# Converting stored fp64 weights with fewer steps, with their range checked in later blocks and one set of operands made later

## The chip, the cores and the metric

The kernel runs on one core of a Trainium2 chip. The metric is the time of one execution in microseconds (us) of the device. The core has TensorE (PE, matmuls; PEld is its weight load), VectorE (DVE), ScalarE (ACT), GpSimd (POOL) and SyncE (SP), whose queue issues every DMA of this kernel. Each engine works through its own instructions in the order in which they stand.

## The reference

A linear attention with a decaying state feeds an MLP with squared ReLU, and that feeds a mixture of eight experts which are all computed and weighted by a Sinkhorn-normalised gate:

```python
for t in range(S):                                   # 4 batches x 8 heads, S=768, D=48
    state = f[:, :, t, :, None] * state + np.einsum('bhd,bhe->bhde', k[:, :, t], v[:, :, t])
    y[:, :, t] = np.einsum('bhd,bhde->bhe', q[:, :, t], state)
...
h = x @ w_in                                         # 3072 tokens, 384 -> 2048
r = np.maximum(h, 0.0)
return (r * r) @ w_out                               # 2048 -> 384
...
P = np.exp(logits - logits.max())                    # logits = x @ w_gate, 8 columns
for _ in range(8):
    P /= P.sum(1, keepdims=True) + 1e-09
    P /= P.sum(0, keepdims=True) + 1e-09
    P *= N / E
for e in range(E):
    out += P[:, e:e+1] * (np.maximum(x @ w1[e], 0.0) @ w2[e])   # 384 -> 1024 -> 384
```

The MLP's weights `w_in` and `w_out` arrive as raw 64-bit floating-point words; the kernel turns them into fp32 by integer operations on the two 32-bit halves of each word.

## The kernel before

**Tiling.** The 3072 tokens form 8 blocks of 384. A block is made by three chunks of attention (c = 0 to 23), and its MLP has 16 f-steps. Step i = 16*block + f multiplies the block's `x` with a slice of `w_in` (**e1**, products_in: L713 in block 0, in fp32; L717 later, nine matmuls of high and low parts), ACT takes ReLU (L722), square (L725) and the rounded high part (L729), DVE the low part (**lo**, L733), and **e2** (m_out, L742 in block 0, L746 later) multiplies with a slice of `w_out`. e1 runs a few steps ahead of e2. The gate's logits follow each block. From about 530 us to the end the experts run (L983, L1045).

**Attention of a chunk**: two scans of the decay (L400, L407), products of q and k with them (**mulk** L412, **mulq** L416, on DVE for the first chunks, on POOL later), the turn of k on PE (ktr, L474) and its copy by ACT (Kn, L478), scores (pp), causal mask (QP, L464 or L469), state (S, Sh), then the **MIX** on PE (L537, L546 or L553, into y). ACT and DVE write the result as high and low part into `x` (L593 or L597; DVE's part, **yl**, is L595). When a block's third chunk is written, **spread** (L603) has SP issue six small DMAs x<-x; the first e1 of that block needs them. SP also issues state moves (L438, vt<-Sh), query moves (L443, QP<-kq) and the loads of the chunks.

**Conversion of the weights.** There are 16 groups `wm[n]` of 128 x 768 words, 768 KB each, loaded into slots `raw`. Group n is needed at step n of block 0. In order: ACT takes the magnitude of the high halves (L1362, `Abs`, cv_t<-raw), ACT scales the low halves (L1365), DVE clamps the magnitude to the range that fp32 can hold (L1370, r<-cv_t), DVE masks and shifts the fields (L1375), DVE puts the sign in (L1379), POOL adds the halves (**total**, L1383), and ACT and DVE split the fp32 result for the later blocks (L335, L338). The load of a later group waits until a total has freed a slot.

**Operands of the experts (xb).** After a block's MLP, DVE makes sums of parts of its output (L875), ACT rounds them (L882), DVE takes the rest (L886), and SP writes 15 results per block to memory (L891, xd<-xb). They are wanted only from about 500 us on.

**What sets the order.** Every piece of work is a step of a `Plan`, with an engine, a duration that the program assumes, a due time and the steps it needs. A list scheduler in the program orders all steps once, by the assumed times; the result is the fixed order on each engine. Steps in `plan.soft` give way to others. Where PE would stand idle early, it places matmuls named `warm` that compute nothing needed. The slots of 768 KB (`rawp`) are handed on in the order of a list `users`: the last groups of weights, then the operands of the blocks, then the experts' weights.

Of the kernel before, what the change touches and what calls it, by code (L numbers as in the profile page):

```python
# [38 lines left out]
TB = 512  # L39
# [40 lines left out]
class Plan:  # L80
# [15 lines left out]
    def add(self, name, eng, dur, due, fn, needs=(), lag=0.0, start=0.0):  # L96
        assert name not in self.steps, name
        self.steps[name] = (eng, dur, due, fn, [n for n in needs if n is not None], lag, start)

    def load(self, name, kb, due, fn, needs=(), n=1, start=0.6, rate=350.0):  # L100
        self.add(name + ("issue",), "sp", 0.48 * n, due, fn, needs, start=start)
        self.add(name, "dma", kb / rate, due, lambda: None, [name + ("issue",)], lag=1.2)
# [77 lines left out]
def body(tc, fkq, v, wm, wa, wc, gate, seqs, out):  # L180
# [49 lines left out]
    def if_(ok, name):  # L230
        return name if ok else None
# [92 lines left out]

    def cv_abs(n):
        cvt[n] = cvp.tile([128, KD, TB // 2 + 1], F32, tag="t", name="cv_t")
        R[n] = wb.tile([128, WCOL], F32, tag=f"b{n}", name="r")
        F64(nc, cvt[n][:, :, 0:TB // 2], raws[n], R[n]).magnitude()

    def cv_total(n):  # L330
        F64(nc, cvt[n][:, :, 0:TB // 2], raws[n], R[n]).total(R[n])

# [7 lines left out]
    for n in range(NF):  # L340
        part = lambda m, n=n: getattr(F64(nc, cvt[n][:, :, 0:TB // 2], raws[n], R[n]), m)()
# [8 lines left out]
        plan.off_port |= {("cvb", n, 0), ("cvb", n, 1)}  # L350
# [248 lines left out]
    def spread(blk):  # L599
        X = x1[blk].bitcast(F32)  # L600
        for j in range(2):
            for k in range(KD):
                sp.dma_start(out=X[64 * j + DH:64 * j + 64, :, k, :], in_=X[64 * j + 16 * k:64 * j + 16 * k + 16, :, NP - 1, :])  # L603

    moved = []
    for c in range(NCH):
# [478 lines left out]

    last_pe = None

    users = [("cv", n, [("cvs", n)]) for n in late[-2:]]
    users += [("xb", j, [("xbo", j, o) for o in ROW_OPS]) for j in range(NB - 1)]
    for g in range(NSTEP):  # L1090
        users += [("wa", g, [("w2lo", g, 0), ("w2lo", g, 1), ("wsum", g, 5)]), ("wc", g, [("w2lo", g, 2), ("w2lo", g, "c")])]
    slot_of = {}
    for n in range(2, len(users)):
        prev = users[n - 1]
        slot_of[users[n][:2]] = users[n - 2][2] + ([] if n == 2 else [("ld" + prev[0], prev[1], "issue")])

    for j in range(NB):
# [229 lines left out]
    def in_range():  # L1327
        dve.tensor_reduce(out=mx, in_=minf, axis=AX.XY, op=ALU.min)
        dve.tensor_scalar(out=mx, in0=mx, scalar1=MIN_DECAY, scalar2=None, op0=ALU.is_lt)

    def in_range_all():
# [5 lines left out]

    add("range", "dve", 0.3, n1 - 12, in_range, [("scanf", NCH - 1)])
    add("rangeall", "pool", 3.5, n1 - 11, in_range_all, ["range"])
# [9 lines left out]
class F64:  # L1349

    def __init__(self, nc, t, raw, flat=None):
        self.nc, self.t, self.flat = nc, t, flat
        self.high = raw.bitcast(I32).rearrange("p (n two) -> p n two", two=2)[:, :, 1]
        self.word = raw.bitcast(U32).rearrange("p (n two) -> p n two", two=2)[:, :, 0]

    def like(self, a):
        return a.rearrange("p (a b) -> p a b", a=KD) if self.flat is not None else a

    def magnitude(self):
        self.nc.scalar.activation(out=self.t, in_=self.like(self.high.bitcast(F32)), func=ACTF.Abs)  # L1362

# [3 lines left out]
    def clamp(self):  # L1367
        dve, t = self.nc.vector, self.t
        out = t if self.flat is None else self.like(self.flat)
        dve.tensor_scalar(out=out, in0=t, scalar1=F64_LOW, scalar2=F64_HIGH, op0=ALU.max, op1=ALU.min)  # L1370

    def fields(self):
        dve, ti = self.nc.vector, self.t.bitcast(I32)
        src = ti if self.flat is None else self.like(self.flat.bitcast(I32))
        dve.tensor_scalar(out=ti, in0=src, scalar1=0x07FFFFFF, scalar2=3, op0=ALU.bitwise_and, op1=ALU.logical_shift_left)  # L1375

# [265 lines left out]
```

## Time and profile before

| | us |
|---|---|
| median of three runs (1982.39 to 1984.84) | 1982.9 |
| profiled execution, its own time | 1984.72 |
| its span | 1982.7 |
| PE busy | 1964.8 |
| DVE busy | 1399.0 |
| POOL busy | 972.4 |
| ACT busy | 908.5 |

The span is the time from the first to the last record of the profiled execution; about 2 us of its own time lie around it. PE is busy for 99% of the span, and its granted clock is 0.998 on average. What PE loses lies in a few places, each of which can be read in the timeline as an idle time with the name of what ended it.

### The profile page before, as it was taken

The page shows a single profiled execution, that of the slowest core. Times are in us where ns is not written, and L with a number is a line of the kernel's source. Part 1 is how long each engine was busy: PE and PEld are TensorE (multiplying, and loading weights), DVE is VectorE, ACT ScalarE, POOL GpSimd, SP SyncE. Part 2 cuts the span into 40 slices and gives each one's busy share as a digit, 9 for nine tenths or more (in the row PEclk, how much of TensorE's full clock was granted, in tenths as well). Part 3 has the DMA queues.
Part 4 walks back from the last instruction along what each step waited for, and adds up shares of the span by engine and source line. Part 5 has one row for each costly group of instructions (what it writes and reads, how often), then busy time and mean ns, then how long its engine had stood idle before and what let it go on. Part 6 is the DMA issues. An engine that isn't in the chain of part 4 may idle for free.

```text
span 1982.7 us, 29656 instructions
## 1 busy us (share of the span) xinstructions
PE 1964.8 (99%) x10921; PEld 1665.1 (84%) x10921; DVE 1399.0 (71%) x2314; ACT 908.5 (46%) x1643; POOL 972.4 (49%) x915
## 2 busy tenths in 40 slices
PE   8999999999999999999999999999999999999998
PEld 6699999999988888888888888888888888888887
DVE  8987666752577777666777777676677777766676
ACT  6665555655644443333444443433444444333342
POOL 2520111100245667776665556646666556666661
PEclk9999999999999999999999999999999999999999
DMA  7524343425202111121111114411111011111101
GB/s 267 179 77 115 106 111 100 111 70 188 79 33 66 49 53 58 59 67 48 57 33 48 33 49 161 142 32 57 33 55 49 32 48 33 56 40 48 40 24 50
DMA packets 102322, 146.61 MB, mean 74 GB/s; under 512 B 23608, under 2 KB 71320, under 8 KB 102168
## 3 DMA queue, kind: packets, MB, share of 16 engines
q1 hardware_dynamic: 102168, 144.63, 23.2%
q8 instruction: 88, 1.44, 0.3%
q14 instruction: 66, 0.54, 0.1%
HBM read 115.42 MB, written 21.14 MB: 69 GB/s over the span
## 4 chain that ended last, share of the span: by engine, by line
PE 94%; DVE 4%; issue 1%; DMA 1%; ACT 0%; SPq 0%; DVEq 0%; ACTq 0%
PE o L1045 40%; PE e L983 33%; PE a L746 8%; PE e L717 8%; PE a L742 1%; PE e L713 1%; PE y L553 1%; PE lg L761 1%; DVE sg L400 1%; PE pp L492 0%; PE pp L453 0%; PE ktr L474 0%; DVE QP L464 0%; DVE cv_t L1375 0%; DVE r L1370 0%
## 5 line engine op out<-in xcount | busy, mean ns | idle before, releaser
L1045 PE MATMUL o<-h,w 128*128 128x512 f32 x3456 | 790.7, 389 | 0.0
L1045 PEld LDWEIGHTS o<-h,w 128*128 128x128 f32 x3456 | 648.3, 188 | 135.0
L983 PE MATMUL e<-x,w 128*128 128x512 f32 x2304 | 536.2, 390 | 0.2 <-DVE vt L1010 0.2
L983 PEld LDWEIGHTS e<-x,w 128*128 128x128 f32 x2304 | 430.0, 188 | 94.5 <-DVE vt L1006 2.4
L1081 POOL TENSOR_TENSOR acc<-acc,sc 128x512 f32<-128x512 f32 x252 | 388.0, 1548 | 129.8 <-DVE sc L1072 126.6
L1072 DVE TENSOR_TENSOR sc<-o,pb 128x512 f32<-128x512 f32 x261 | 179.3, 687 | 213.6 <-PE o L1045 209.0
L934 ACT CAST w<-rawa 128x640 fp32r<-128x640 f32 x128 | 89.8, 726 | 285.3 <-DMA rawa<-in_wa_dram 142.7
L1010 DVE TENSOR_TENSOR v<-v,e 128x512 f32<-128x512 f32 x256 | 174.8, 683 | 64.5 <-PE e L983 57.8
L717 PE MATMUL e<-x,w 128*128 128x384 f32 x1008 | 193.5, 337 | 2.0 <-DMA x<-x 1.8
L934 ACT CAST w<-rawc 128x640 fp32r<-128x640 f32 (+1 forms) x128 | 97.2, 782 | 209.1 <-PE o L1045 157.9
L938 DVE TENSOR_TENSOR w<-rawa,w 128x640 fp32r<-128x640 f32 x128 | 152.6, 1211 | 57.2 <-ACT w L934 57.1
L1029 POOL TENSOR_TENSOR h<-vt,h 128x512 fp32r<-128x512 f32 x64 | 83.5, 1305 | 199.6 <-ACT vt L1024 197.4
L717 PEld LDWEIGHTS e<-x,w 128*128 128x128 f32 x1008 | 175.8, 188 | 3.8 <-ACT xb L882 2.0
L746 PE MATMUL a<-hi,w 128*128 128x384 f32 x672 | 173.9, 339 | 0.0
L1029 POOL TENSOR_TENSOR h<-v,h 128x512 fp32r<-128x512 f32 x64 | 82.8, 1295 | 154.3 <-ACT v L1024 77.7
L733 DVE TENSOR_TENSOR lo<-g,hi 128x384 fp32r<-128x384 f32 x112 | 74.9, 674 | 110.3 <-ACT hi L729 107.3
L1003 ACT ACTIVATE v<-e 128x512 f32<-128x512 f32 x128 | 76.3, 596 | 155.9 <-PE e L983 117.7
L1010 DVE TENSOR_TENSOR vk<-vk,e 128x512 f32<-128x512 f32 x192 | 131.8, 687 | 18.2 <-PE e L983 0.2
L983 PE MATMUL e<-xr,w 128*128 128x512 f32 x576 | 143.2, 392 | 0.1
L412 POOL TENSOR_TENSOR kq<-kq,sg 128x512 f32<-128x512 f32 x18 | 21.5, 1195 | 237.5 <-DVE sg L400 157.8
L983 PEld LDWEIGHTS e<-xr,w 128*128 128x128 f32 x576 | 106.9, 188 | 24.9 <-DVE v L1010 1.6
L938 DVE TENSOR_TENSOR w<-rawc,w 128x640 fp32r<-128x640 f32 (+1 forms) x128 | 120.8, 946 | 9.7 <-ACT w L934 9.5
(144 smaller groups left out, 2371.1 us busy)
## 6 DMA issues: line engine op xcount, KB each, us to landing
rawa<-in_wa_dram SPq DMA_DIRECT2D x64, 384.0 KB
rawc<-in_wc_dram SPq DMA_DIRECT2D x64, 384.0 KB
xd<-xb SPq DMA_DIRECT2D x120, 128.0 KB
raw<-in_wm_dram SPq DMA_DIRECT2D x16, 768.0 KB
x<-xd SPq DMA_DIRECT2D x24, 512.0 KB
pb<-ptd SPq DMA_DIRECT2D x16, 768.0 KB
kq<-in_fkq_dram SPq DMA_DIRECT2D x23, 512.0 KB
fraw<-in_fkq_dram SPq DMA_DIRECT2D x24, 256.0 KB
```

Source lines behind the costliest of these rows:

```text
L717: pe.matmul(ps, w[wl][:, k * 128:(k + 1) * 128], xx[:, xl, k, :], start=n == 0, stop=n == 3 * KD - 1)
L733: dve.tensor_tensor(out=lo, in0=g, in1=hi.bitcast(F32), op=ALU.subtract)
L746: pe.matmul(acc1[j][m], W[f][wl][:, D + m * 128:D + (m + 1) * 128], g, start=f == 0 and n == 0, stop=f == NF - 1 and n == 2)
L934: act.copy(out=W2[g, k][:, 0, 0:n], in_=src)
L938: dve.tensor_tensor(out=W2[g, k][:, 1, 0:n], in0=src, in1=W2[g, k][:, 0, 0:n].bitcast(F32), op=ALU.subtract)
L983: pe.matmul(bank[g, c], w[a], x[:, b], start=o == CHAIN[c][0] and n == 0, stop=n == 2, skip_group_check=True)
L1003: act.activation(out=t, in_=c, func=ACTF.Copy, scale=-1.0)
L1010: dve.tensor_tensor(out=t, in0=t, in1=c, op=op)
L1029: pool.tensor_tensor(out=h[:, 1], in0=hid_src(g, o), in1=h[:, 0].bitcast(F32), op=ALU.subtract)
L1045: pe.matmul(ob[q, t, m], w[:, a, c:c + 128], h[:, b], start=half == f == n == 0, stop=half == f == 1 and n == 2)
L1072: dve.tensor_tensor(out=dst, in0=ob[q, t, m], in1=pbt[p, e][:, t * TB:(t + 1) * TB], op=ALU.mult)
L1081: eng.tensor_tensor(out=acc[p, t, m], in0=acc[p, t, m], in1=sc[q, t, m], op=ALU.add)
```

## The change

Five things change together.

1. **Conversion**: magnitude and clamp are gone. DVE takes the raw high halves directly, shifts them by three bits and masks them (`shifted`, L1416), puts the sign in (L1420); ACT's scaling of the low half and POOL's total stay. So per group one ACT and one DVE instruction less.
2. **Range check in blocks 2 to 5**: since nothing is clamped any more, each group of words is loaded again (`ldchk`, L1123, 768 KB into a slot `chk`), ACT takes the magnitude in place (L1400), and DVE takes the largest and the smallest of each row (L1428, twice). Four groups per block, one after the other in the same slot: the load of a group waits for the second reduction of the one before. `in_range` joins the results by six more small instructions and so decides, with the test it held already, on the general path of the kernel.
3. **XB0_AT = 152**: the operands of block 0 may start only at 152 in the plan's time.
4. **Planned cost of a DMA issue** 0.64 instead of 0.48 (loads, xd writes), and 3.84 instead of 3.0 for a spread. These are numbers of the plan only; they move instructions.
5. The planned costs of the conversion's steps change, and the scheduler orders everything anew.

```diff
+XB0_AT = 152.0
...
     def load(self, name, kb, due, fn, needs=(), n=1, start=0.6, rate=350.0):
-        self.add(name + ("issue",), "sp", 0.48 * n, due, fn, needs, start=start)
+        self.add(name + ("issue",), "sp", 0.64 * n, due, fn, needs, start=start)
...
-        add(("cva", n), "act", 0.75, due, lambda n=n: cv_abs(n), [("ldw", n), if_(n >= 3, ("cvs", n - 3))], start=CV_AT + CV_STEP * n)
-        add(("cvw", n), "act", 0.74, due, lambda p=part: p("low"), [("ldw", n), ("cva", n)])
-        add(("cvb", n, 0), "dve", 0.88, due, lambda p=part: p("clamp"), [("cva", n)])
-        add(("cvb", n, 1), "dve", 0.88, due, lambda p=part: p("fields"), [("cvb", n, 0)])
-        add(("cvb", n, 2), "dve", 0.96, due, lambda p=part: p("sign"), [("cvb", n, 1)])
+        add(("cvw", n), "act", 0.9, due, lambda n=n: F64(nc, None, raws[n]).low(), [("ldw", n)], start=CV_AT + CV_STEP * n)
+        add(("cvb", n, 1), "dve", 0.93, due, lambda n=n: cv_shift(n), [("ldw", n), if_(n >= 3, ("cvs", n - 3))], start=CV_AT + CV_STEP * n)
+        add(("cvb", n, 2), "dve", 0.93, due, lambda n=n: fields(n).sign(), [("cvb", n, 1)])
...
-            add(("sprd", blk), "sp", 3.0, g + to(3, 0.5), lambda blk=blk: spread(blk), [("yl", c - i) for i in range(CPB)], lag=2.2)
+            add(("sprd", blk), "sp", 3.84, g + to(3, 0.5), lambda blk=blk: spread(blk), [("yl", c - i) for i in range(CPB)], lag=2.2)
...
+    SPAN_AT = {j: range(NF // 4 * (j - 1), NF // 4 * j) for j in range(1, 5)}
...
+    for j in range(NB - 1):
+        users.append(("xb", j, [("xbo", j, o) for o in ROW_OPS]))
+        if j in SPAN_AT:
+            users.append(("span", j, [("span", n, 1) for n in SPAN_AT[j]]))
...
+        for k, n in enumerate(group):
+            d = (j + 1) * NF + 2.2 + 3.2 * k
+            plan.load(("ldchk", n), 786, d, lambda j=j, n=n: sp.dma_start(out=chk[j], in_=wm[n]), [prev])
+            for m, (key, eng) in enumerate(((0, "act"), (2, "dve"), (1, "dve"))):
+                plan.soft.add(("span", n, key))
...
-        soft = lambda name, eng, dur, d, fn, needs: (plan.soft.add(name), add(name, eng, dur, d, fn, needs))
+        soft = lambda name, eng, dur, d, fn, needs, start=0.0 if j else XB0_AT: (plan.soft.add(name), add(name, eng, dur, d, fn, needs, start=start))
...
-            add(("xbo", j, o, "issue"), "sp", 0.48, due(n) + 0.2, lambda j=j, o=o: xb_out(j, o), [("xbl", j, o)])
+            add(("xbo", j, o, "issue"), "sp", 0.64, due(n) + 0.2, lambda j=j, o=o: xb_out(j, o), [("xbl", j, o)])
...
+    def shifted(self):
+
+        dve, ti = self.nc.vector, self.t.bitcast(I32)
+        dve.tensor_scalar(out=ti, in0=self.like(self.high), scalar1=3, scalar2=0x3FFFFFFF, op0=ALU.logical_shift_left, op1=ALU.bitwise_and)
...
+    def largest(self, out, least):
+        h = self.high.bitcast(F32)
+        self.nc.vector.tensor_reduce(out=least if out is None else out, in_=h, axis=AX.X, op=ALU.min if out is None else ALU.max)
```

What the scheduler makes of it is shown at three places; the names carry the numbers of buffers, which differ between the two kernels, and line numbers are higher by three after the change.

The head of the MLP, on PE, before and then after: e are the first steps' e1, a their e2, ktr the turn of k for chunk 3.

```order
L713 MATMUL e_459<-x_301,r 128x384 x3
L713 MATMUL e_471<-x_301,r 128x384 x3
L284 MATMUL warm<-shift 128x128 x2
L742 MATMUL a_493<-g,r 128x384
L742 MATMUL a_494<-g,r 128x384
L742 MATMUL a_495<-g,r 128x384
L713 MATMUL e_506<-x_301,r 128x384 x3
L474 MATMUL ktr<-shift,kq_117 128x128 x4
```

```order
L716 MATMUL e_459<-x_304,r 128x384 x3
L716 MATMUL e_471<-x_304,r 128x384 x3
L716 MATMUL e_484<-x_304,r 128x384 x3
L745 MATMUL a_495<-g,r 128x384
L745 MATMUL a_496<-g,r 128x384
L745 MATMUL a_497<-g,r 128x384
L716 MATMUL e_511<-x_304,r 128x384 x3
L477 MATMUL ktr<-shift,kq_119 128x128 x4
```

The third e1 now stands where warm matmuls stood, and a fourth e1 stands ahead of chunk 3's ktr, where there was the third. On DVE, the stretch between the mask of chunk 2 and the product kq that this ktr needs, before and after:

```order
L469 TENSOR_TENSOR QP_126<-pp,mask 128x512 x2
...
L1370 TENSOR_SCALAR r<-cv_t 128x768
L1379 SCALAR_TENSOR_TENSOR cv_t<-raw_222,cv_t 128x3x256
...
L400 SCALAR_TENSOR_TENSOR sg_121<-sg_121,d_122 128x516
L401 TENSOR_SCALAR d_122<-sg_121 128x4
L402 RECIPROCAL d_122<-d_122 128x4
L1375 TENSOR_SCALAR cv_t<-r 128x3x256
L1370 TENSOR_SCALAR r<-cv_t 128x768
L1375 TENSOR_SCALAR cv_t<-r 128x3x256
L1379 SCALAR_TENSOR_TENSOR cv_t<-raw_225,cv_t 128x3x256
L412 TENSOR_TENSOR kq_117<-kq_117,sg_121 128x512
```

```order
L472 TENSOR_TENSOR QP_128<-pp,mask 128x512 x2
...
L1420 SCALAR_TENSOR_TENSOR cv_t<-raw_246,cv_t 128x3x256
L1416 TENSOR_SCALAR cv_t<-raw_419 128x3x256
...
L403 SCALAR_TENSOR_TENSOR sg_123<-sg_123,d_124 128x516
L404 TENSOR_SCALAR d_124<-sg_123 128x4
L405 RECIPROCAL d_124<-d_124 128x4
L1416 TENSOR_SCALAR cv_t<-raw_463 128x3x256
L415 TENSOR_TENSOR kq_119<-kq_119,sg_123 128x512
```

Between the scan's reciprocal and the product stood four steps of the conversion; now one does, the shift of group 5. Between the mask and the scan stood eight steps of the conversion, now there are seven.

The turn from block 1 to block 2, on SP, before and after: the x<-x are spread(2).

```order
L891 DMA xd_14_134<-xb 256x1x128
L443 DMA QP_127<-kq_117 48x4x64 x2
L891 DMA xd_13_137<-xb 256x1x128
L443 DMA QP_127<-kq_117 48x4x64 x2
L891 DMA xd_11_138<-xb 256x1x128
L603 DMA x_1296<-x_1296 16x2x384 x6
L891 DMA xd_12_139<-xb 256x1x128
L438 DMA vt_123<-Sh 48x192 x2
```

```order
L380 DMA fraw_117<-in_fkq_dram 128x512
L388 DMA vt_127<-in_v_dram 64x384 x2
L446 DMA QP_128<-kq_120 48x4x64 x2
L606 DMA x_1258<-x_1258 16x2x384 x6
L894 DMA xd_6_133<-xb 256x1x128
L894 DMA xd_7_134<-xb 256x1x128
L894 DMA xd_8_135<-xb 256x1x128
L894 DMA xd_14_136<-xb 256x1x128
L894 DMA xd_4_137<-xb 256x1x128
L441 DMA vt_125<-Sh 48x192 x2
```

All writes of block 0's operands now stand behind spread(2); eight stood ahead of it. On PE the last MIX of block 2 has six steps (three e1, three e2) behind it before the first e1 of block 2, where four stood.

Block 3, on SP, before and after: the moves of states and queries around a check's load.

```order
L443 DMA QP_127<-kq_119 48x4x64 x4
L385 DMA vt_123<-in_v_dram 64x384 x2
L891 DMA xd_3_144<-xb 256x1x128
L438 DMA vt_124<-Sh 48x192 x2
L438 DMA vt_125<-Sh 48x192 x2
L891 DMA xd_1_145<-xb 256x1x128
L380 DMA kq_118<-in_fkq_dram 128x1024
```

```order
L446 DMA QP_129<-kq_121 48x4x64 x4
L388 DMA vt_125<-in_v_dram 64x384 x2
L441 DMA vt_126<-Sh 48x192 x2
L1123 DMA chk<-in_wm_dram 128x768
L441 DMA vt_127<-Sh 48x192 x2
L383 DMA kq_120<-in_fkq_dram 128x1024
```

A load of a check, which waits for the reduction of the check before, now stands between the two state moves that a MIX needs. From the first e1 of block 2 to the end the order on PE is the same in both kernels.

## Rows read from the trace of the kernel before

**Rows 1.** The page, its chain of work that ended last, by engine.

```profile
PE 94%; DVE 4%; issue 1%; DMA 1%; ACT 0%; SPq 0%; DVEq 0%; ACTq 0%
```

**Rows 2.** Waits of PE: line waiting, releaser, us in total, times, longest.

```profile
PE ktr L474 <- DVE kq L412: 2.2, 2, 1.5
PE e L717 <- DMA x<-x: 1.8, 1, 1.8
...
PE y L553 <- ACT g L722: 1.6, 2, 0.9
PE a L746 <- DVE lo L733: 0.9, 1, 0.9
...
PE e L717 <- DVE x L595: 0.3, 1, 0.3
```

**Rows 3.** Timeline of PE, head: start, duration, instruction, idle time before and releaser.

```profile
28.62 4.11 PE L713 MATMUL e<-x,r 128*128 128x384 f32 x12
32.56 0.61 PE L284 MATMUL warm<-shift 128*128 128x128 f32 x4
33.61 2.20 PE L742 MATMUL a<-g,r 128*128 128x384 f32 x6 [0.45 <-ACT g L725]
...
39.24 0.66 PE L474 MATMUL ktr<-shift,kq 128*128 128x128 f32 x4 [1.49 <-DVE kq L412]
```

**Rows 4.** Timeline of DVE, head.

```profile
35.72 0.94 DVE L1370 TENSOR_SCALAR r<-cv_t 128x768 f32<-128x768 f32 x1
...
38.50 0.68 DVE L412 TENSOR_TENSOR kq<-kq,sg 128x512 f32<-128x512 f32 x1
```

**Rows 5.** Timeline of ACT, head: the magnitude that waits for the load of group 5.

```profile
36.16 0.92 ACT L1362 ACTIVATE cv_t<-raw 128x768 f32<-128x768 f32 x1 [1.66 <-DMA raw<-in_wm_dram]
```

**Rows 6.** Groups by line, operation and form: xcount, busy us, mean ns.

```profile
L1379 DVE SCALAR_TENSOR_TENSOR cv_t<-raw,cv_t 128x768 int32<-128x768 int32 x16 | 15.7, 999 | 0.1
...
L1370 DVE TENSOR_SCALAR r<-cv_t 128x768 f32<-128x768 f32 x16 | 15.1, 944 | 0.6 <-ACT cv_t L1362 0.6
...
L1427 DVE TENSOR_REDUCE sk_cs<-P 128x8 f32<-128x192 f32 x8 | 4.1, 518 | 1.1 <-POOL P L1424 1.1
```

**Rows 7.** Timeline of PE, turn from block 1 to block 2.

```profile
168.39 2.57 PE L717 MATMUL e<-x,w 128*128 128x384 f32 x9 [1.75 <-DMA x<-x]
170.76 0.84 PE L746 MATMUL a<-hi,w 128*128 128x384 f32 x2
...
173.24 1.72 PE L717 MATMUL e<-x,w 128*128 128x384 f32 x9
174.80 0.51 PE L746 MATMUL a<-hi,w 128*128 128x384 f32 x2
...
176.36 0.85 PE L717 MATMUL e<-x,w 128*128 128x384 f32 x4
```

**Rows 8.** Timeline of all engines, same turn: the last yl and spread.

```profile
159.50 0.74 DVE L595 TENSOR_TENSOR x<-y,x 128x256 fp32r<-128x256 f32 x2
...
164.19 3.82 SPq L603 DMA_DIRECT2D x<-x  x6
```

**Rows 9.** Windows: PE, PEld, DVE, ACT, POOL busy us (instructions), PE clock, DMA share, GB/s.

```profile
10.00:20.00 10.00, 9.54 (x102) 7.60 (x98) 9.79 (x22) 5.86 (x12) 0.00 (x0) 1.00 1.03 408
...
166.00:174.00 8.00, 6.25 (x27) 5.70 (x26) 5.80 (x15) 3.60 (x10) 2.37 (x2) 0.79 0.41 93
175.00:235.00 60.00, 59.37 (x584) 58.01 (x583) 40.99 (x109) 35.37 (x83) 7.44 (x6) 1.00 0.47 128
```

**Rows 10.** Timeline of all engines, the middle of block 2.

```profile
199.25 1.20 POOL L412 TENSOR_TENSOR kq<-kq,sg 128x512 f32<-128x512 f32 x1 [27.34 <-DVE sg L400]
...
199.49 1.37 DVE L733 TENSOR_TENSOR lo<-g,hi 128x384 fp32r<-128x384 f32 x1
```

**Rows 11.** Timeline of SP, turn from block 2 to block 3: its spread.

```profile
223.13 4.82 SPq L603 DMA_DIRECT2D x<-x  x6
```

**Rows 12.** Timeline of PE, same turn: the first e1 of block 3.

```profile
231.36 1.72 PE L717 MATMUL e<-x,w 128*128 128x384 f32 x9
```

More of the change, by code (lines that the diff above doesn't have):

```diff
@@ L201, in body @@
     flag = const.tile([128, 1], I32, name="flag")
+    span = const.tile([128, 2, NF], F32, name="span")
+    ends = const.tile([128, 2], F32, name="ends")
     sk = Sinkhorn(nc, const)
@@ L323, in ldw, with fields, cv_shift, cv_total @@
         sp.dma_start(out=raws[n], in_=wm[n])
-    def cv_abs(n):
+    def fields(n):
+        return F64(nc, cvt[n][:, :, 0:TB // 2], raws[n], KD)
+    def cv_shift(n):
         cvt[n] = cvp.tile([128, KD, TB // 2 + 1], F32, tag="t", name="cv_t")
+        fields(n).shifted()
+    def cv_total(n):
         R[n] = wb.tile([128, WCOL], F32, tag=f"b{n}", name="r")
-        F64(nc, cvt[n][:, :, 0:TB // 2], raws[n], R[n]).magnitude()
-    def cv_total(n):
-        F64(nc, cvt[n][:, :, 0:TB // 2], raws[n], R[n]).total(R[n])
+        fields(n).total(R[n])
     def cv_hi(n):
@@ L340, in body @@
     for n in range(NF):
-        part = lambda m, n=n: getattr(F64(nc, cvt[n][:, :, 0:TB // 2], raws[n], R[n]), m)()
         due = n - LEAD_W
         plan.load(("ldw", n), 786, LOADS["w"] + n if n < 4 else due - 3, lambda n=n: ldw(n), [if_(before(n) >= 0, ("cvs", before(n)))], start=W_AT)
-        add(("cva", n), "act", 0.75, due, lambda n=n: cv_abs(n), [("ldw", n), if_(n >= 3, ("cvs", n - 3))], start=CV_AT + CV_STEP * n)
-        add(("cvw", n), "act", 0.74, due, lambda p=part: p("low"), [("ldw", n), ("cva", n)])
-        add(("cvb", n, 0), "dve", 0.88, due, lambda p=part: p("clamp"), [("cva", n)])
-        add(("cvb", n, 1), "dve", 0.88, due, lambda p=part: p("fields"), [("cvb", n, 0)])
-        add(("cvb", n, 2), "dve", 0.96, due, lambda p=part: p("sign"), [("cvb", n, 1)])
+        add(("cvw", n), "act", 0.9, due, lambda n=n: F64(nc, None, raws[n]).low(), [("ldw", n)], start=CV_AT + CV_STEP * n)
+        add(("cvb", n, 1), "dve", 0.93, due, lambda n=n: cv_shift(n), [("ldw", n), if_(n >= 3, ("cvs", n - 3))], start=CV_AT + CV_STEP * n)
+        add(("cvb", n, 2), "dve", 0.93, due, lambda n=n: fields(n).sign(), [("cvb", n, 1)])
         add(("cvs", n), "pool", 1.95, due, lambda n=n: cv_total(n), [("cvb", n, 2), ("cvw", n)])
-        plan.off_port |= {("cvb", n, 0), ("cvb", n, 1)}
+        plan.off_port.add(("cvb", n, 1))
         gone = [(s, k) for k in left_by(n) for s in ("e2", "cvl")]
@@ L1086, in body @@
     last_pe = None
+    SPAN_AT = {j: range(NF // 4 * (j - 1), NF // 4 * j) for j in range(1, 5)}
     users = [("cv", n, [("cvs", n)]) for n in late[-2:]]
-    users += [("xb", j, [("xbo", j, o) for o in ROW_OPS]) for j in range(NB - 1)]
+    for j in range(NB - 1):
+        users.append(("xb", j, [("xbo", j, o) for o in ROW_OPS]))
+        if j in SPAN_AT:
+            users.append(("span", j, [("span", n, 1) for n in SPAN_AT[j]]))
     for g in range(NSTEP):
@@ L1095, in body, with span_new, span_of @@
         slot_of[users[n][:2]] = users[n - 2][2] + ([] if n == 2 else [("ld" + prev[0], prev[1], "issue")])
+    chk = {}
+    def span_new(j):
+        chk[j] = rawp.tile([128, WCOL], I64, tag="raw", name="chk")
+    def span_of(j, n, k):
+        w = F64(nc, None, chk[j])
+        if k == 0:
+            w.magnitude(w.high.bitcast(F32))
+        elif k == 1:
+            w.largest(None, span[:, 1, n:n + 1])
+        else:
+            w.largest(span[:, 0, n:n + 1], None)
+    for j, group in SPAN_AT.items():
+        add(("ldspan", j, "issue"), "none", 0, (j + 1) * NF + 1, lambda j=j: span_new(j), slot_of["span", j])
+        prev = ("ldspan", j, "issue")
+        for k, n in enumerate(group):
[3 more added lines that the diff above has]
+                plan.soft.add(("span", n, key))
+                add(("span", n, key), eng, 0.92, d + 1 + 0.1 * m, lambda j=j, n=n, key=key: span_of(j, n, key), [("ldchk", n) if m == 0 else ("span", n, 0 if m == 1 else 2)])
+            prev = ("span", n, 1)
     for j in range(NB):
@@ L1329, in in_range @@
         dve.tensor_scalar(out=mx, in0=mx, scalar1=MIN_DECAY, scalar2=None, op0=ALU.is_lt)
+        dve.tensor_reduce(out=ends[:, 0:1], in_=span[:, 0], axis=AX.X, op=ALU.max)
+        dve.tensor_reduce(out=ends[:, 1:2], in_=span[:, 1], axis=AX.X, op=ALU.min)
+        dve.tensor_scalar(out=ends[:, 0:1], in0=ends[:, 0:1], scalar1=F64_HIGH, scalar2=None, op0=ALU.is_gt)
+        dve.tensor_scalar(out=ends[:, 1:2], in0=ends[:, 1:2], scalar1=F64_LOW, scalar2=None, op0=ALU.is_lt)
+        dve.tensor_tensor(out=mx, in0=mx, in1=ends[:, 0:1], op=ALU.max)
+        dve.tensor_tensor(out=mx, in0=mx, in1=ends[:, 1:2], op=ALU.max)
     def in_range_all():
@@ L1336, in choose @@
         general.append(nc.values_load(flag[0:1, 0:1], min_val=0, max_val=1))
-    add("range", "dve", 0.3, n1 - 12, in_range, [("scanf", NCH - 1)])
+    add("range", "dve", 1.0, n1 - 12, in_range, [("scanf", NCH - 1)] + [("span", n, 1) for n in range(NF)])
     add("rangeall", "pool", 3.5, n1 - 11, in_range_all, ["range"])
@@ L1349, with __init__ @@
 class F64:
-    def __init__(self, nc, t, raw, flat=None):
-        self.nc, self.t, self.flat = nc, t, flat
+    def __init__(self, nc, t, raw, parts=None):
+        self.nc, self.t, self.parts = nc, t, parts
         self.high = raw.bitcast(I32).rearrange("p (n two) -> p n two", two=2)[:, :, 1]
@@ L1358, in like, with magnitude @@
     def like(self, a):
-        return a.rearrange("p (a b) -> p a b", a=KD) if self.flat is not None else a
-    def magnitude(self):
-        self.nc.scalar.activation(out=self.t, in_=self.like(self.high.bitcast(F32)), func=ACTF.Abs)
+        return a if self.parts is None else a.rearrange("p (a b) -> p a b", a=self.parts)
+    def magnitude(self, out=None):
+        self.nc.scalar.activation(out=self.t if out is None else out, in_=self.high.bitcast(F32), func=ACTF.Abs)
     def low(self):
@@ L1368, in clamp @@
         dve, t = self.nc.vector, self.t
-        out = t if self.flat is None else self.like(self.flat)
-        dve.tensor_scalar(out=out, in0=t, scalar1=F64_LOW, scalar2=F64_HIGH, op0=ALU.max, op1=ALU.min)
+        dve.tensor_scalar(out=t, in0=t, scalar1=F64_LOW, scalar2=F64_HIGH, op0=ALU.max, op1=ALU.min)
     def fields(self):
         dve, ti = self.nc.vector, self.t.bitcast(I32)
-        src = ti if self.flat is None else self.like(self.flat.bitcast(I32))
-        dve.tensor_scalar(out=ti, in0=src, scalar1=0x07FFFFFF, scalar2=3, op0=ALU.bitwise_and, op1=ALU.logical_shift_left)
+        dve.tensor_scalar(out=ti, in0=ti, scalar1=0x07FFFFFF, scalar2=3, op0=ALU.bitwise_and, op1=ALU.logical_shift_left)
+    def shifted(self):
+        dve, ti = self.nc.vector, self.t.bitcast(I32)
+        dve.tensor_scalar(out=ti, in0=self.like(self.high), scalar1=3, scalar2=0x3FFFFFFF, op0=ALU.logical_shift_left, op1=ALU.bitwise_and)
     def sign(self):
```

## The prediction

> **What bounds the kernel now.** I read first the chain of work that ended last: 94% of it is PE [rows 1], and the table of the case gives PE 1964.8 of 1982.7 us of span. So a change off PE is worth only what PE loses now. I read that from the list of PE's waits: a few waits, each seen once or twice, and none of the large ones after the first 300 us [rows 2]. Three places answer to the parts of the change.
>
> *The head.* PE runs two e1 from 28.62 to 32.56, 2.06 us per step by 4.11 for two. Then warm matmuls fill the time until the first e2 at 33.61, which waits for ACT's square; that is 1.05 us. The ktr of chunk 3 then waits 1.49 us for DVE's product kq [rows 3]. After 39.24 I found no gap on PE up to about 135 us.
>
> *The turn from block 1 to block 2.* One e2 waits 0.9 for DVE's lo, one e1 0.3 for yl [rows 2], and the first e1 of block 2 waits 1.75 for spread(2). Behind that wait PE runs slower: the nine e1 from 168.39 to 170.76 take 2.37 us where the nine from 173.24 to 174.80 take 1.56, and six e2 from 170.76 to 173.24 take 2.48 where those from 174.80 to 176.36 take 1.56 [rows 7]. That is 0.81 + 0.92 = 1.73 us more. The windows show the granted clock: 0.79 from 166 to 174, and 1.00 in the 60 us behind [rows 9]. PE had been idle just ahead of the fall, and the idle time is the wait for spread.
>
> *Blocks 2 to 5.* Two MIXes of blocks 2 and 3 wait for ACT's ReLU, 1.6 together, the longer 0.9 [rows 2]. PE is busy 59.37 of 60 us there, DVE 40.99, ACT 35.37 [rows 9].
>
> **The change, part by part.**
>
> *Conversion.* Each group loses a magnitude on ACT and a clamp on DVE, 16 clamps of 0.944 us, 15.1 in all [rows 6]. The shift reads raw words with a stride; the sign step, which reads the same words, takes 0.999 [rows 6]. So I take about 0.95 to 1.0 for the shift, as for the step that it replaces. What counts is where a DVE step stood ahead of something that PE waits for. Ahead of chunk 3's kq, four conversion steps fewer stand on DVE (one between mask and scan, three behind the reciprocal). DVE ran that stretch without a gap, so kq moves from 38.50 [rows 4] to about 38.50 - 4 x 0.95 = 34.7. One thing can hold it: the shift of group 5 stands right ahead and needs its load, whose words were there at 36.16 [rows 5]. If that load comes no earlier, shift and kq end at 36.16 + 0.95 + 0.68 = 37.8. PE now has a third e1, an e2 and a fourth e1 ahead of the ktr: 32.56 + 3 x 2.06 = 38.7. Either way ktr does not wait, and the third e1 fills the 1.05. The head gives **2.54 us**. The bounds: nothing, if the totals of groups 2 to 5 on POOL come too late for the e1 that now stand earlier; 2.54 is all that is lost there, so it can't be more. I take all, since the sign step of each of these groups also has fewer steps ahead of it.
>
> *Block 0's operands later.* They leave DVE, ACT and SP around 130 to 165 us. The order on SP shows eight writes that stood ahead of spread(2) gone, and PE has two more steps between the last MIX of block 2 and the first e1. Now, yl ends at 160.24 and SP comes to spread only at 164.19 [rows 8], 3.95 us later. PE waits 1.75 for it. One query move (two issues) is left ahead of it, two steps of 1.56 more lie behind the MIX. So spread can begin some 2 us earlier and is needed 3.1 us later: the wait goes, and with it the dip of the clock. lo at the turn then has no operand sums around it. The turn gives 0.9 + 0.3 + 1.75 + 1.73 = **4.7 us**. Its bounds: 3.48 (wait for spread and dip alone) and 4.7.
>
> *The checks.* 16 loads, 16 magnitudes on ACT, 32 reductions on DVE. The trace has no reduction of 768; the strided one of 192 takes 0.518 [rows 6], four times that is 2.07; a strided pass over 768 words takes 0.999. I take 1.0, since a pass over the same words is nearest. That is 8 us of DVE in each of four blocks, on 40.99 of 60: 82%, at 2.07 93%. The magnitude, 0.92 [rows 5], is 3.7 us of ACT on 35.37. So neither engine becomes the bound by its sum. What it can cost is order: a ReLU behind a magnitude that waits for its load, a lo behind a reduction. PE's e2 stand some steps behind their e1, and most of it is hidden. The MIX is where PE is near its limit now, twice in the twelve of blocks 2 to 5. I put as much again on top, **+1.6 us**; the bounds are 0 and 12 MIXes x 0.8 (the mean of the two) = 9.6, less the 1.6 that is there already: 8.0.
>
> Here a rule speaks for the lower end. The lo that began at 199.49, while POOL's multiplication ran to 200.45, took 1.37 us [rows 10]. If reductions were held by POOL in that way, each by at most the whole 1.20 of one of six multiplications a block [rows 9, 10], DVE would have 7.2 us more, no more than the upper price of a reduction gives already. The Trainium skill (SBUF — State Buffer, Who interferes with whom) says that a VectorE instruction with two SBUF inputs contends with a GpSimd instruction that reads SBUF, and that a reduction never does on trn2. By it the sum has no such 7.2 us; it moves neither bound.
>
> *Planned cost of issues, and the six operations of the range test.* They are numbers for the scheduler, or lie off PE's path; from block 2 on PE's order is the same. Nothing, if their cover holds: DVE's share in the expert stage is small against PE's, and the general path's decision is taken late.
>
> **The sum.** The profiled execution took 1984.72: 1984.72 - 2.54 - 4.7 + 1.6 = 1979.1. That execution stood 1.8 above the median, so for the median 1982.9 - 5.6 = **1977.3 us**. A time within 0.2% (4.0 us) of before can hardly be told from no change, so faster means under 1978.9.
>
> **The rivals.**
>
> *The checks eat the gain.* ACT and DVE take their work in order. With all of block 0's operands now in block 2 beside the first checks, DVE there comes near 90%. If eight or so of the twelve MIXes wait 0.8 instead of four, that is 5 us, and the time is 1982.9 - 7.2 + 5 = 1980.7. For it speaks that both present MIX waits come from ACT standing behind work for operands; against it that later turns already carry operands and lose nothing at spread. The same time comes out if the head gives nothing (1979.8).
>
> *No new wait.* The checks are hidden altogether, and the two MIX waits go as the order shifts: 1982.9 - 7.2 - 1.6 = 1974.1.
>
> *Slower: SP held by the checks.* A check's load waits for the second reduction of the one before, and SP does nothing else meanwhile. Behind it stand state moves and, a few rows on, the spread of the next block. In the turn from 2 to 3 spread starts at 223.13, takes 1.0 longer than at the turn before [rows 8, 11], and the e1 needs it at 231.36 [rows 12]. At the turn before, 4.20 us lay between spread's start and the e1 that waited for it [rows 7, 8], so the slack is 231.36 - 223.13 - 5.2 = 3.0 us. If SP is held some 5 us longer at four turns, each costs what the turn to block 2 costs now, 1.75 + 1.73 = 3.5, so 14 in all: 1982.9 - 7.2 + 14 = 1989.7. It decides from about 2.8 us a turn on, for 7.2 + 4.0 = 11.2. Against it: reductions of 1 us can't be 5 us late unless the load itself is.
>
> Here a rule speaks against the change. At full load the queues moved 408 GB/s [rows 9], by which 768 KB take 1.93 us. The Trainium skill (DMA: Bandwidth & Descriptors, Queues, rings and completion order) says that on each DMA engine descriptors are consumed in ring order. By that a spread or a state move issued right behind a check's load would land up to 1.93 us later. For spread, whose load stands five rows ahead, it is inside the 3.0 us; a state move stands right behind a check's load, so it is the one that may show it. No run here shows a small transfer behind a large one.
>
> **How the numbers follow.** The forecast, within 2 us: 0.50. No new wait: 0.15. Checks eat the gain, or the head gives nothing: 0.25. Slower: 0.10. The forecast's own span crosses 1978.9 only at its upper end, so of its 0.50 I give 0.46 to faster; with the 0.15, **faster 0.61**; same 0.25 + 0.04 = 0.29; slower 0.10. The range goes from 1973.8, just under the case with no new wait, to 1984.5, the dearest check case (1975.7 + 8.0 = 1983.7) and a little; the slower case lies outside.
>
> **What the profile after would show.** Right: ktr of chunk 3 without a wait and no warm matmuls between the second and third e1; no wait for x<-x and a clock of 1.00 around 160 to 175; at MIX, four waits or so for ReLU. The shift at 0.95 to 1.0, the reduction near 1.0. Wrong: an e1 of block 0 that waits for a total of POOL (head); lo or ReLU waits in block 2 beside the operands; SP waiting on the reduction for several us with a state move or a spread behind it, or a clock under 1 at a later turn; a reduction near 2 us.

## The result

The changed kernel takes 2009.06 us (median of four, 2007.86 to 2012.63) against 1983.38 for the kernel before (1982.39 to 1984.84): a ratio of 1.0132, interval 1.0114 to 1.0149. It is 1.3% slower. The forecast was 1977.3, with a range up to 1984.5, and "slower" had a chance of 0.10 for a reason that isn't the one found.

The waits that the prediction spoke of are gone. PE's waits in the changed kernel:

```profile
PE warm L287 <- POOL shift L256: 1.7, 1, 1.7
PE ds L502 <- ACT Kn L481: 0.9, 3, 0.3
PE y L556 <- ACT g L725: 0.9, 1, 0.9
PE a L749 <- ACT x2t L756: 0.8, 2, 0.4
PE pp L462 <- DVE kq L419: 0.6, 1, 0.6
...
PE ktr L477 <- DVE kq L415: 0.3, 1, 0.3
```

There is no wait for x<-x any more, nor for lo, and one MIX waits 0.9 where two waited 1.6 [rows 2]. The head, on the timeline of PE:

```profile
7.17 0.66 PE L477 MATMUL ktr<-shift,kq 128*128 128x128 f32 x4 [0.34 <-DVE kq L415]
...
29.62 5.00 PE L716 MATMUL e<-x,r 128*128 128x384 f32 x15
34.46 2.10 PE L745 MATMUL a<-g,r 128*128 128x384 f32 x6
36.39 2.10 PE L716 MATMUL e<-x,r 128*128 128x384 f32 x6
38.33 0.60 PE L477 MATMUL ktr<-shift,kq 128*128 128x128 f32 x4
39.56 1.16 PE L462 MATMUL pp<-kq 48*128 48x128 f32 x16 [0.63 <-DVE kq L419]
```

Three e1, e2, e1 and chunk 3's ktr follow each other without a wait, where warm matmuls and 1.49 us of waiting stood [rows 3]; the ktr that waits 0.3 is that of the first chunk. The step behind chunk 3's ktr waits 0.63. At the turn to block 2, the windows, and the timelines of DVE and SP:

```profile
160.00:168.00 8.00, 8.00 (x47) 8.00 (x46) 7.55 (x18) 4.27 (x11) 2.71 (x2) 1.00 0.42 115
175.00:235.00 60.00, 60.00 (x589) 58.78 (x588) 47.05 (x112) 38.31 (x89) 7.73 (x6) 1.00 0.64 186
```

```profile
153.58 0.75 DVE L598 TENSOR_TENSOR x<-y,x 128x256 fp32r<-128x256 f32 x2
...
155.10 3.81 SPq L606 DMA_DIRECT2D x<-x  x6
159.01 3.24 SPq L894 DMA_DIRECT2D xd<-xb  x5
```

PE is full and its clock 1.00, where it was 0.79 over the 8 us around the turn [rows 9]; spread goes out at 155.10 instead of 164.19 [rows 8], right behind a yl that begins at 153.58 instead of 159.50, with the operands' writes behind it.

So where do the 25 us come from that it is slower? PE is busy 1993.5 us instead of 1964.8: it doesn't wait more, its matmuls take longer. The groups by line, before:

```profile
L1045 PE MATMUL o<-h,w 128*128 128x512 f32 x3456 | 790.7, 389 | 0.0
L983 PE MATMUL e<-x,w 128*128 128x512 f32 x2304 | 536.2, 390 | 0.2 <-DVE vt L1010 0.2
L983 PE MATMUL e<-xr,w 128*128 128x512 f32 x576 | 143.2, 392 | 0.1
```

and in the changed kernel:

```profile
L1048 PE MATMUL o<-h,w 128*128 128x512 f32 x3456 | 813.1, 395 | 0.0
L986 PE MATMUL e<-x,w 128*128 128x512 f32 x2304 | 537.6, 391 | 0.2
L986 PE MATMUL e<-xr,w 128*128 128x512 f32 x576 | 146.4, 398 | 0.1
```

The same 3456 matmuls of the experts' second product take 22.4 us more, the 576 on xr 3.2 more, and the 2304 on x 1.4 more. The clock isn't it; windows of o<-h,w alone (columns: PE, PEld, clock, DMA), before and after:

```profile
1000.00:1090.00 90.00, 49.32 (x216) 40.55 (x216) 1.00 0.14 44
```

```profile
1000.00:1090.00 90.00, 50.73 (x216) 40.54 (x216) 1.00 0.14 44
```

216 matmuls at full clock take 1.41 us longer, 6.5 ns each; their weight loads take the same. Counted by the starts of the records, a matmul of h and w follows the last after 226.9 ns before and 233.3 after (means within unbroken runs).

The lead of one execution over that of the kernel before, at the same matmul and counted from the first matmul of each, shows when the time goes (us; negative is ahead; worked out from starts in the traces; the last row counts the matmuls from 0; a_gap96 and the others are experiments below):

```
at                      changed  a_gap96  a_gap96_nochk  a_gap96_xb0  b_sp64_xb0  a_gap96_sp48
e1 of step 16            -2.43    -3.06      -3.17         -2.75        +0.07        -2.45
e1 of step 32 (block 2)  -5.67    -6.74      -6.85         -5.43        -3.60        -6.13
e1 of step 48 (block 3)  -6.39    -7.38      -6.99         -6.64        -2.52        -2.09
e1 of step 60            -6.90    -8.23      -6.99         -7.48        -2.52        -2.95
e1 of step 112           -3.71    -5.21      -5.28         -6.27        -0.79        -1.15
first o<-h,w             -2.99    -5.26      -3.72         -4.71        -0.81        -1.17
o<-h,w no. 2592         +17.48    -3.91      -2.83         -3.75        +1.35        -0.95
```

The changed kernel is 6.9 us ahead in block 3, loses 3 of it by the end of block 6 (1 at one MIX, 2 evenly over the steps), and then about 1.7 us in every 90 us of the expert stage.

What changed for those matmuls is where their operands lie. The change has two new tiles, `span` (128 bytes a partition) and `ends` (8, kept as 32), in the first pool on the left of SBUF. Every tile behind them on that side starts 160 bytes later; those on the right stay. From the built programs:

```
start address        before   changed
w (experts, left)      4832      4992
x (left)              78560     78720
h (right)            167904    167904
xr (right)           217056    217056
h - w, modulo 256         0        96
xr - w, modulo 256        0        96
x - w, modulo 256         0         0
```

The two forms that slowed are those whose distance changed. The MLP shows it inside one trace: its x and hi lie on the right, and the weights of steps f = 8 to 13 of a block too, those of the others on the left. In the changed kernel the nine matmuls of an e1 with weights on the left start 176 to 177 ns after one another (median), those with f = 8 to 13 at 173 to 174.5; before, all are at 173 to 174.

### The profile page after: what moved, and what is told of

It is laid out like the page before. It is cut to its first block, busy times and chain, and to the rows that moved or that the text cites. A ratio compares the mean times of both kernels' runs of the same rounds, so it can differ in the third digit from the quotient of the medians.

```text
span 2006.9 us, 29716 instructions
## 1 busy us (share of the span) xinstructions
PE 1993.5 (99%) x10919; PEld 1669.4 (83%) x10919; DVE 1421.3 (71%) x2336; ACT 909.6 (45%) x1643; POOL 977.5 (49%) x915
## 4 chain that ended last, share of the span: by engine, by line
PE 95%; DVE 2%; DMA 1%; ACT 1%; issue 0%; SPq 0%; DVEq 0%; ACTq 0%
PE o L1048 40%; PE e L986 33%; PE a L749 8%; PE e L720 8%; PE a L745 1%; PE e L716 1%; PE y L556 1%; PE lg L764 1%; PE pp L495 1%; PE ktr L477 0%; PE pp L456 0%; DMA raw<-in_wm_dram 0%; DVE sg L403 0%; DMA chk<-in_wm_dram 0%; DMA fraw<-in_fkq_dram 0%
## 5 line engine op out<-in xcount | busy, mean ns | idle before, releaser
L1048 PE MATMUL o<-h,w 128*128 128x512 f32 x3456 | 813.1, 395 | 0.0
L736 DVE TENSOR_TENSOR lo<-g,hi 128x384 fp32r<-128x384 f32 x112 | 70.2, 629 | 101.5 <-ACT hi L732 100.5
```

The costliest lines, as they stand in the source:

```text
L736: dve.tensor_tensor(out=lo, in0=g, in1=hi.bitcast(F32), op=ALU.subtract)
L1048: pe.matmul(ob[q, t, m], w[:, a, c:c + 128], h[:, b], start=half == f == n == 0, stop=half == f == 1 and n == 2)
```

## The experiments

Each adds an unused tile, changes numbers of the plan or leaves the checks out, or does two of these, and is otherwise the kernel that it starts from. "a" starts from the changed kernel, "b" from the one before.

**32 bytes more in the changed kernel, 32 bytes alone in the one before, and the checks away.**

```diff
     ends = const.tile([128, 2], F32, name="ends")
+    const.tile([128, 8], F32, name="gap")        # a_gap32, a_gap32_nochk
...
     flag = const.tile([128, 1], I32, name="flag")
+    const.tile([128, 8], F32, name="gap")        # b_gap32
...
+    edge = ctx.enter_context(tc.tile_pool(name="edge", bufs=1, side="right"))
+    edge.tile([128, 8], F32, name="gap")         # a_right32
     x1e = ctx.enter_context(tc.tile_pool(name="x1e", bufs=1, side="right", reuse_waits="tile"))
...
-    SPAN_AT = {j: range(NF // 4 * (j - 1), NF // 4 * j) for j in range(1, 5)}
+    SPAN_AT = {}                                 # a_gap32_nochk
```

> The changed kernel with one unused tile of 32 bytes behind `ends`, so that the tiles on the left of SBUF stand 192 bytes, not 160, from where they stood before. Placement theory (a matmul is slower when its weights and its moving operand start in different halves of 64 bytes: the new tiles moved the weights on the left from 32 to 0 in 64, h, xr and x1 on the right stayed at 32): the matmuls of h and w fall back from 231 to 238 ns to 227, and the time is 1983.4 less the lead of 6.9 us that the changed kernel had at step 60, so 1976 to 1979. Schedule theory (the new order, or traffic that the checks or the new order cause, slows the matmuls; no address matters): 2009, as the order is the same.

> The kernel before with one unused tile of 32 bytes behind `flag`, nothing else. Placement theory: the weights on the left start at 0 in 64, h, xr and x1 at 32; the matmuls of h and w go from 227 to 231 to 238 ns, and what the changed kernel lost against its lead (from 6.9 ahead to 24 behind, 31 us) is lost here: 2012 to 2016. Schedule theory: 1983.4.

> The changed kernel with one unused tile of 32 bytes at the right end of SBUF, so that every tile on the right (h, xr, x1, hi, lo) starts 32 bytes lower, at 0 in 64, as the weights on the left now do. If what counts is how weights and moving operand lie to each other: 1976 to 1979. If it is where the weights on the left lie by themselves (0 is slow, 32 fast): 2009. Schedule theory: 2009.

> As a_gap32, and the range check left out: no second load of the weights, no magnitudes, no reductions, and the test of the decay alone decides. Placement theory, with the prediction's step that the checks cost 1.6 us: 1.6 under a_gap32. If the checks are hidden, as the lead of 6.9 us at step 60 says: within 1 us of a_gap32. If the checks' traffic is what slows the matmuls: 1976 here, and 2009 for a_gap32.

Measured, against 1984.05: a_gap32 1996.59 (1.0057, 1.0040 to 1.0073), b_gap32 2009.31 (1.0124, 1.0107 to 1.0141), a_right32 1996.69 (1.0058, 1.0041 to 1.0074), a_gap32_nochk 1997.76 (1.0067, 1.0050 to 1.0084).

The group of o<-h,w in b_gap32:

```profile
L1046 PE MATMUL o<-h,w 128*128 128x512 f32 x3456 | 813.0, 396 | 0.0
```

An unused tile of 32 bytes makes the kernel before as slow as the changed one: no order, no check, no conversion is needed for it (2012 to 2016 was expected, some 3 us too much). The same 32 bytes take 12.5 us off the changed kernel, and leaving out the checks, with the six operations of the range test, changes nothing clear of noise. So the schedule theory falls. The placement theory as I had stated it, by halves of 64 bytes, falls too: a_gap32 has both operands at 32 modulo 64 again and is still 12.5 us slower than the kernel before. a_gap32 and a_right32 have different addresses but the same distance from w to h, 64 modulo 256, and they agree in time within 0.1 us and in pitch, the mean time from one start of o<-h,w to the next (230.9 and 230.8 ns). That pointed to the distance.

**The distance put back from either side, and other distances.**

```diff
+    const.tile([128, 24], F32, name="gap")       # a_gap96, a_gap96_nochk: behind ends
...
+    edge.tile([128, 24], F32, name="gap")        # a_right96
...
+    const.tile([128, 16], F32, name="gap")       # b_gap64: behind flag
...
+    const.tile([128, 32], F32, name="gap")       # b_gap128: behind flag
```

> The changed kernel with an unused tile of 96 bytes behind `ends`: the left tiles stand 256 bytes from where they stood before, so the distance from a weight tile on the left to h or xr on the right is again a multiple of 256, as it was before. Distance theory (the matmuls' pitch hangs on that distance: 227 ns at 0, 231 at 64, 233 at 96 and at 224, as the four kernels so far show): matmuls of h and w at 227 throughout, and the lead of 7 us at step 60 stays: 1976 to 1979. Half-line theory (only the offset in 64 bytes counts): as a_gap32, 1996.6. Schedule theory (what is left of a_gap32's loss is the order's doing): 1996.6.

> The changed kernel with the left as it is and an unused tile of 96 bytes at the right end, so that every tile on the right starts 96 bytes lower and the distance is a multiple of 256 again. Distance theory: 1976 to 1979, as a_gap96. If the place of the left tiles by itself matters: about 2009, or 1997.

> The kernel before with an unused tile of 64 bytes behind `flag`; the distance is 192 in 256, the offsets within 64 bytes are those of before. Distance theory: pitch about 231 as at 64, and about 18 to 20 us more than before, 2001 to 2004. Half-line theory: 1984, as before.

> As a_gap96, and the range check left out: no second load of the weights, no magnitudes, no reductions; the test of the decay alone decides. The prediction's step (checks cost 1.6 us, bounds 0 and 8): 1.6 under a_gap96. If they are hidden: within 1 us of a_gap96. If the list order that the checks shift is worth more than their work: it can come out above a_gap96.

> The kernel before with an unused tile of 128 bytes behind `flag`; the distance from the weights on the left to h and xr is 128 in 256. If the pitch repeats every 128 bytes: as before, 227 ns and 1984 to 1985. If only a multiple of 256 is as fast as before: 230 to 234 ns and 1996 to 2012.

Measured: a_gap96 1981.55 (0.9983, 0.9974 to 0.9992), a_right96 1981.43 (0.9984, 0.9974 to 0.9993), a_gap96_nochk 1982.60 (0.9987, 0.9978 to 0.9996), b_gap64 2011.95 (1.0133, 1.0117 to 1.0148), all against 1984.86; b_gap128 2010.78 against 1984.47 (1.0134, 1.0118 to 1.0149). The groups of o<-h,w in a_gap96, a_right96 and b_gap128:

```profile
L1049 PE MATMUL o<-h,w 128*128 128x512 f32 x3456 | 790.7, 389 | 0.0
```

```profile
L1050 PE MATMUL o<-h,w 128*128 128x512 f32 x3456 | 790.6, 389 | 0.0
```

```profile
L1046 PE MATMUL o<-h,w 128*128 128x512 f32 x3456 | 811.2, 395 | 0.0
```

With the distance at a multiple of 256 again, reached from the left or from the right, the matmuls are back at 790.6 to 790.7, and the changed kernel beats the one before by 3.3 us. (1976 to 1979 was expected of both: the lead of 7 us at step 60 isn't kept, as the table of leads shows.) Distances of 64 and 128 aren't enough, and b_gap64, at 192, came out dearer than the 2001 to 2004 expected from the runs at 64: the distance doesn't count alike in both directions. Pitch of o<-h,w by distance modulo 256: 226.9 at 0, 230.9 at 64, 233.3 at 96, 232.8 at 128, 233.4 at 192, 233.3 at 224.

**One operand alone.** All these moved a whole side. In two kernels only h, and only x, moves among the operands of matmuls.

```diff
+        new("edge", 1, side="right").tile([128, 8], F32, name="gap")   # b_hgap32
         pools["h"] = new("h2p", 1, side="right")
...
         pools["x"] = ctx.enter_context(tc.tile_pool(name="xp", bufs=1, reuse_waits="tile"))
+        pools["x"].tile([128, 8], F32, name="gap")                     # b_xgap32
```

> The kernel before with an unused tile of 32 bytes at the right, ahead of the pool of h alone: h (and the sums below it) starts 32 bytes lower, the weights, xr and the operands x stay. If the distance between the two operands of a matmul sets its own pitch: o<-h,w at 233 (distance 224), e<-xr,w and e<-x,w at 228 as before, and 3456 x 6.5 ns = 22 us more, 2006 to 2008. If what counts is where left and right lie as a whole, or what other engines read and write meanwhile: all three forms change, or none.

> The kernel before with an unused tile of 32 bytes ahead of the operands x on the left: their distance from the weights, a multiple of 256 in every kernel so far, becomes 32. Operand theory: e<-x,w, at 228 in every kernel so far, goes to 231 to 234, 2304 x 3 to 6 ns = 7 to 14 us more, 1992 to 1999; o<-h,w stays at 227. If that form is fast for another reason: 1984 to 1985.

Measured, against 1983.45: b_hgap32 2007.53 (1.0120, 1.0103 to 1.0137), b_xgap32 1997.15 (1.0065, 1.0048 to 1.0082). Groups of b_hgap32, then one of b_xgap32:

```profile
L1046 PE MATMUL o<-h,w 128*128 128x512 f32 x3456 | 813.0, 396 | 0.0
...
L984 PE MATMUL e<-x,w 128*128 128x512 f32 x2304 | 536.2, 390 | 0.2 <-DVE vt L1011 0.2
```

```profile
L984 PE MATMUL e<-x,w 128*128 128x512 f32 x2304 | 549.7, 396 | 0.2
```

With h moved, o<-h,w takes 813.0 and e<-x,w stays at 536.2. With x moved, e<-x,w, which never slowed before, takes 549.7. Each of these two forms goes by the distance of its own two operands. One thing is not explained: in b_xgap32 the matmuls on xr, whose distance is unchanged, slow too, about half as much (228.4 to 231.3 ns from start to start); each nine of them stand behind 36 on x.

**The parts of the schedule, at the distance of before.** Three runs undo one part of the change or do two of its parts alone, so that the prediction's steps can be read. The last edit stands for b_sp64_xb0, which has the planned costs of 0.64 and 3.84 besides; a_gap96_sp48 has the old ones for the loads, the writes of operands (0.48) and spread (3.0).

```diff
-XB0_AT = 152.0
+XB0_AT = 0.0                                     # a_gap96_xb0
...
-        self.add(name + ("issue",), "sp", 0.64 * n, due, fn, needs, start=start)
+        self.add(name + ("issue",), "sp", 0.48 * n, due, fn, needs, start=start)   # a_gap96_sp48
...
-        soft = lambda name, eng, dur, d, fn, needs: (plan.soft.add(name), add(name, eng, dur, d, fn, needs))
+        soft = lambda name, eng, dur, d, fn, needs, start=0.0 if j else 152.0: (plan.soft.add(name), add(name, eng, dur, d, fn, needs, start=start))
```

> As a_gap96, with XB0_AT = 0, so that block 0's operands may start as early as before. By the prediction's step (the turn to block 2 is worth 4.7 us, 3.5 at least, and comes from the later operands): a wait for spread(2) and a fall of the clock come back, 1984.5 to 1986. If the shorter conversion alone makes room for the operands: no wait at the turn, and 1981 to 1982 as a_gap96.

> The kernel before with XB0_AT = 152 and the planned cost of issues alone: magnitude and clamp stay, nothing is checked, no tile is new. By the prediction: the turn's 4.7 us without the head's 2.5, 1980 against 1984.9. If the turn needs the shorter conversion: no change.

> As a_gap96, with the planned cost of issues put back (0.48, and 3.0 for a spread). The prediction gave this part nothing: within 1 us of a_gap96. If it orders SP so that waits appear: 2 us and more above.

Measured, against 1984.47: a_gap96_xb0 1981.88 (0.9988, 0.9979 to 0.9997), b_sp64_xb0 1986.48 (1.0017, 1.0008 to 1.0026), a_gap96_sp48 1983.64 (0.9994, 0.9985 to 1.0003).

*The later operands are not what the turn needs.* Without them a_gap96_xb0 has no wait at the turn and is ahead by 6.6 us at block 3, though twelve writes of block 0's operands stand ahead of spread(2), where eight stood in the kernel before. The last of them, on SP:

```profile
148.64 4.06 SPq L895 DMA_DIRECT2D xd<-xb  x4
...
154.87 3.94 SPq L607 DMA_DIRECT2D x<-x  x6
```

With them and without the shorter conversion b_sp64_xb0 wins 3.6 us up to the turn too, but loses it again and misses the 1980 expected. From the turn to 420 us, PE's waits in it are these:

```profile
PE y L553 <- ACT g L722: 3.2, 4, 1.0
PE a L746 <- ACT x2t L753: 1.8, 1, 1.8
```

Four MIXes wait for ReLU, 3.2 us together (1.6 before), and an e2 1.8 us for ACT's copy of block 1's result.

*The planned cost of an issue, priced at nothing, has a price.* a_gap96_sp48 is 6.8 ahead at step 40 and 2.1 at step 41. ACT's timeline at that place, then PE's:

```profile
198.49 0.88 ACT L1401 ACTIVATE chk<-chk 128x768 f32<-128x768 f32 x1 [3.70 <-DMA chk<-in_wm_dram]
199.27 0.47 ACT L726 ACTIVATE g<-e 128x384 f32<-128x384 f32 x1
```

```profile
199.79 1.76 PE L557 MATMUL y<-QP,vt 128*64 128x64 f32 x28 [2.68 <-ACT g L726]
```

A check's magnitude holds ACT for 3.70 us until its load lands; the ReLU behind it is late; the MIX waits 2.68; and the windows show the clock fall behind the idle time, as at the old turn:

```profile
195.00:203.00 8.00, 5.32 (x86) 4.81 (x87) 3.91 (x5) 2.93 (x6) 1.95 (x2) 0.75 0.36 115
203.00:211.00 8.00, 8.00 (x55) 7.85 (x50) 7.21 (x17) 3.56 (x7) 1.19 (x1) 0.82 0.62 170
```

So one badly placed check costs 4.7 us, and the longer planned issues keep it from happening in the order of the changed kernel. In times the two kernels are 2.1 us apart, but their intervals overlap; one trace is the evidence here.

## Why the prediction was wrong

**The step that failed.** "They are numbers for the scheduler, or lie off PE's path; from block 2 on PE's order is the same. Nothing, if their cover holds." This put the range test at nothing. I costed the instructions of the check, and not the two tiles that hold its results. With the order on PE unchanged I took every matmul's duration from the trace of before. But 160 bytes of new tiles moved the weights against h and xr, and 3456 + 576 matmuls became longer by 6 ns, 25.6 us by the groups; the MLP's steps with weights on the left lost about 2 more. Experiments show it from both sides: 32 bytes alone bring the loss, 96 bytes take it away.

**The rival that it slows.** SP held by the checks, 1989.7. It didn't happen: PE waits for no spread. SP is held by the checks, the load of one waiting for the reduction of the one before:

```profile
SPq L1123 <- DVE span L1428: 7.9, 5, 3.3
```

But that is 7.9 us between 170 and 420 us, at most 3.3 at a time, and no wait of PE is for a spread or a state move. That the kernel is slower fits this rival by accident only.

**The head, 2.54.** Right in the main: 2.4 us ahead at step 16, 3.1 in a_gap96. Chunk 3's ktr doesn't wait, as forecast; the step behind it waits 0.63 in the changed kernel and not at all in a_gap96. That 3.1 lies above the bound of 2.54; what the other half microsecond is stays open.

**The turn, 4.7 (3.48 to 4.7).** Right in size, 3.8 us between steps 24 and 36 (2.08 to 5.85 ahead); the wait for x<-x and the dip are gone. Its cause was put wrong: I gave it to the later operands, left yl where it was and let spread begin some 2 us earlier. In the trace yl ends at 154.33 instead of 160.24 and spread begins 0.8 us behind it instead of 3.95, so 9.1 us earlier. Between the same steps a_gap96_xb0 gains 4.4 us without the later operands, a_gap96_sp48 4.4 with the old planned costs, and b_sp64_xb0 3.0 without the shorter conversion, each without the wait. So none of the three is needed when the other two are there. Whether one alone is enough, no run here shows.

**The checks, +1.6.** Too dear at this order: a_gap96 and a_gap96_nochk are at 5.21 and 5.28 ahead at step 112, and their medians, 1.1 us apart the other way, have overlapping intervals. The waits of the MIX that were to be paid for come without the checks as well (a_gap96, then a_gap96_nochk):

```profile
PE y L557 <- ACT g L726: 1.7, 4, 0.5
```

```profile
PE y L557 <- ACT g L726: 2.9, 4, 0.9
```

The prices of the instructions were nearly right, as DVE's groups in the changed kernel show:

```profile
L1428 DVE TENSOR_REDUCE span<-chk 128x1 f32<-128x768 f32 x32 | 30.1, 947 | 6.9 <-ACT chk L1400 6.9
...
L1416 DVE TENSOR_SCALAR cv_t<-raw 128x768 int32<-128x768 int32 x16 | 15.0, 947 | 1.8 <-DMA raw<-in_wm_dram 1.8
```

0.947 for a reduction where I took 1.0, and 0.947 for the shift where I took 0.95 to 1.0. From 175 to 235 us DVE is busy 47.05 of 60 us, 78%, where it was 40.99 and 82% was worked out. (At 2.07 us a reduction the sum would have been 96%, 40.99 + 8 x 2.07 = 57.55 of 60, and not the 93% of the prediction.) The Trainium skill (SBUF — State Buffer, Who interferes with whom) says that a reduction never contends with GpSimd on trn2. Of the 32 only one ran beside POOL, for 0.79 us of a multiplication; it took 936 ns, where all lie between 936 and 956, and so agrees, as far as one case goes.

**Sum.** Without the shift the forecast's sum, 5.6 us, stands beside 5.3 us of lead at the first matmul of h and w, and 3.3 in the medians of a_gap96. About 1.3 us of that lead goes in the expert stage, most of it in two steps, at which PE waits for DVE's vt (at 623 and 1254 us) as it doesn't in the kernel before. In a_gap96:

```profile
PE e L987 <- DVE vt L1010: 0.7, 2, 0.4
```

b_sp64_xb0 has two such waits too, and loses 2.2 in that stage. Why vt is late there, and where the rest goes, no run here shows.

## What to carry to other kernels

Before pricing a change by the trace of before, ask whether it allocates anything: a small new tile in an early pool moves every tile behind it on its side, and PE can lose more by that than the change is worth, with no wait to show for it. When PE's busy time grows at the same order and clock, compare the mean of each form of matmul, and then the addresses of its operands; an unused tile that restores the old distance is a test of one line. And put work that waits for a load, such as a check off the path, where nothing urgent stands behind it on its engine: one such wait on ACT cost 4.7 us.

## What the hardware showed unexpectedly

A 128x128 by 512 fp32r matmul takes 226.9 ns on average from start to start, in the form o<-h,w, when its weights and its moving operand start a multiple of 256 bytes apart in SBUF, and 230.8 to 233.4 at the six other distances tried (64, 96, 128, 192, 224 modulo 256, and 32 in the form e<-x,w), at full clock and with the same 188 ns of weight load. Moving either operand does it, and moving the other after it undoes it. The exception is xr in b_xgap32, 231.3 ns at a multiple of 256. What inside the chip causes it, no run here shows.
